# A kept block, later turns of grad_out, a fourth step of sums, bf16 spreads and earlier products in a spectral and bilinear layer's forward and backward kernel

## The chip, the core and the metric

The kernel is one program on one core of a Trainium2 chip: one launch computes the forward result and all gradients. The metric is the device time of one execution in microseconds. Three runs of the kernel before gave 1506.52, 1510.41 and 1510.88 us, so the median is 1510.41. A separate execution was profiled. Engine names below: PE is TensorE, DVE is VectorE, ACT is ScalarE, POOL is GpSimd; SP is SyncE, which issues most DMAs. Each engine runs its instructions in the order of its own queue.

## The reference, cut to what matters

```python
def _A_ref(x, w_r, w_i):                     # spectral filter
    X = jnp.fft.rfft2(x.astype(jnp.float32), axes=(-2, -1)) * (w_r + 1j * w_i)
    return jnp.fft.irfft2(X, s=(S, D), axes=(-2, -1)).astype(jnp.bfloat16)

def _B_ref(x, w_gate, w_up, w_down):         # bilinear gated unit, no nonlinearity
    g = jnp.einsum('bsd,df->bsf', x, w_gate)
    u = jnp.einsum('bsd,df->bsf', x, w_up)
    return jnp.einsum('bsf,fd->bsd', g * u, w_down)

mod = (_silu(c) @ w_mod).reshape(1, 6, 1, 576)
sa, ca, ga, sb, cb, gb = (mod[:, i] for i in range(6))
h = _layernorm(x) * (1 + ca) + sa
x = x + ga * _A_ref(h, A_w_r, A_w_i)
h = _layernorm(x) * (1 + cb) + sb
x = x + gb * _B_ref(h, B_w_gate, B_w_up, B_w_down)
```

S = 2048, D = 576, F = 4608, all tensors bf16. The outputs are x and the gradients, by `jax.vjp` with `grad_out`, of x, of the two filter weights, of the three matrices of block B, of c and of w_mod. The gradient of w_mod (`out_8`) is silu(c) times the gradient of each of the six rows of `mod`: six blocks of 576 x 576. The gradient of c is a sum of w_mod times those rows.

## The kernel before, in words

The Fourier transforms are matmuls with tables. Rows of x stand in 16 tiles of 128 (`NT`), F in 36 blocks of 128 (`NFB`), the frequencies in 19 chunks (`NCH`). The stages follow each other, each a software pipeline, whose steps are functions of a tile or chunk: `pipeline(n, [step0, step1, ...])` runs step i on tile k - i in round k.

- **Head and s1**: the six rows of `mod` are made from w_mod by matmuls (`mod_make`; `MSA`, `MCA`, `MGA`, `MSB`, `MCB`, `MGB` number them), with the gate's own column form `gbT` by the small matmuls of L487. `s1_norm`, `s1_cols` and `s1_rows` do the first layernorm and the forward transform. `grad_out` is loaded in three parts, gonA (tiles 0 to 3), gonB (4 to 7) and gonC (8 to 15), and turned on PE (L524), as fillers in this stage; L525 multiplies each turned tile by the gate into `goT`.
- **s2 and s3**: filter, inverse transform, second layernorm (`s3_norm`; L665 and what follows make `h2p`). Between their steps, and after them, run the groups of `u4_group`: for a block of F, ghhT = w_down x goT (L541 to L546), four groups of four row tiles. Groups are numbered; four make block `fb = g // 4`. ACT and DVE evacuate them from PSUM to the SBUF tile `ghh_st`, and after the fourth group POOL stores it to DRAM, `ghhT_d` (L549). The last stretch, 205 to 264.8 us, has these groups alone; at the same time SP and POOL load and transpose what the main loop needs first.
- **Main loop**, 264.8 to about 1215 us: 36 blocks. A block makes gate and up values (`gup`, L799 and L804), loads its ghhT block (`ghh`, L865, pool of two), makes the three products hhT, ggT and guT on DVE (L808 to L810), and from these the gradient of h (`u8p`, L840; its sums on DVE, L843 and L845) and of the weights (`u57p`, L737).
- **t1, t2, t3**: the backward pass through the second layernorm, the spectral block and the first layernorm. Between the steps PE gets fillers, dealt out by hand by `deal`: held matmuls of the weight gradients (`u57p`), then those of the output projection (`u3p`, L1375). `deal` also fixes the order on PE and, in t1, on ACT. `diag` (L1005) collects sums over rows in PSUM, `csA` to `csE`: diagonals are the gradients of the scale rows, an additional column that of the shift rows. `norm_back` (L964 to L974) is the layernorm's backward step; its ScalarE operation is `u` (L964).
- **Tail**: what is left of the projection, 428 matmuls in 16 tiles with `of` (L1388 to L1393) made from each, and six `section`s, one for each row of `mod`: a row's sums are spread over all partitions by fp32 matmuls with ones (`spread`, L1029), copied by ACT (`dmb`, L1048), multiplied by silu(c) on ACT (L1055) and stored to `out_8`, and multiplied by a block of w_mod on DVE (`pr7`, L1061). `late` says at which tile a section starts. `hl` and `hl2` are the projection's operands, loaded by SP; `wd` is w_down, loaded by POOL.

Orders are written out where they matter: `in_order` fixes a list of instructions, `followed(mm, act)` ties a copy to its matmul, `behind` and `queued` keep an instruction behind given ones.

Of the kernel before, what the change touches and what calls it, by code (L numbers as in the profile page):

```python
# [19 lines left out]
NT = 16  # L20
S = 2048
D = 576
# [3 lines left out]
DN = 6 * DS  # L26
# [64 lines left out]
def build(ctx, tc, A_x, A_w_r, A_w_i, B_w_gate, B_w_up, B_w_down, c_in, w_mod, grad_out,  # L91
# [42 lines left out]
    def part(ap):  # L134

        return ap.rearrange("p (m c) -> p m c", m=6)[:, :, 0:DC]

    def parts(ap):

        return ap.rearrange("p t (m c) -> p t m c", m=6)[:, :, :, 0:DC]  # L140
# [5 lines left out]
    def ones_between(ap):  # L146

        nc.gpsimd.memset(ap.rearrange("p t (m c) -> p (t m) c", c=DS)[:, :, DC:DS], 1.0)
# [109 lines left out]
    h2n = h2p[:, :, 0:D]  # L258
    gcms, gons = [], []
# [9 lines left out]
    with ExitStack() as hs:  # L269
# [97 lines left out]
        def wd_load(k):  # L367
            wdn = wdn2[:, k % 2, :, :]
            rows = B_w_down[k * FB4 * 128:(k + 1) * FB4 * 128, :].rearrange("(j f) d -> f j d", f=128)
            nc.sync.dma_start(wdn[:, :, 0:D], rows)  # L370
            nc.sync.dma_start(wdn[:, :, D:DP], rows[:, :, 512:D])
# [79 lines left out]
        hTs, zts = {}, {}  # L451
# [18 lines left out]
        def s1_cols(t):  # L470
# [6 lines left out]
            if t == 3:  # L477
# [8 lines left out]
                for m in range(5):  # L486
                    nc.tensor.matmul(ps[:, 0:1], lhsT=wms[MGB][:, m, D - 128:D], rhs=sc_bf[:, m:m + 1], start=(m == 0), stop=(m == 4))  # L487
# [32 lines left out]
        for t in range(NT):  # L520
            odd = t // 4 % 2
            pt = u4ps.tile([128, 5, 128], BF, name="u4p")
            for m in range(5):
                nc.tensor.transpose(pt[:, m, :], gon(t, m * 128 if m < 4 or not odd else D - 128, 128), ident[:])  # L524
# [4 lines left out]
        def u4_group(g, eng=None):  # L529
            fb, sb4 = g // 4, g % 4  # L530
            k, j = fb // FB4, fb % FB4
# [3 lines left out]
            if sb4 == 0:  # L535
                sts[fb] = (u4w if not u4r or fb % 4 < 2 else u4r[1]).tile([128, NT, 128], BF, name="ghh_st", bufs=2)
# [11 lines left out]
            if sb4 == 3:  # L548
                stored.append(nc.gpsimd.dma_start(ghhT_d[fb * 128:(fb + 1) * 128, :], sts[fb][:].rearrange("f t p -> f (t p)")).ins)  # L549
# [9 lines left out]
        with ExitStack() as rc:  # L559
            c2 = pool("hc2", 2, "right", stack=rc)  # L560
            hwm = pool("hwm", 2, "right", stack=rc)
# [50 lines left out]
            def s2_fill(ci):  # L612
                u4_groups(2)
                if ci == 1:
                    for j in (MGA, MSB):
                        wms[j] = mod_load(j, hwm)
                for j, c0 in ((MGA, 4), (MSB, 7), (MCB, 10)):
                    if ci == c0:
                        mod_make(j, wms[j], "a")
                if ci == 4:  # L620
                    wms[MCB] = mod_load(MCB, hwm)
# [28 lines left out]
        def s3_norm(sa):  # L650
# [13 lines left out]
            nm = hw2.tile([128, 2, D], BF, name="nm", bufs=1)  # L664
            nc.vector.tensor_tensor(out=parts(nm[:]), in0=parts(n2[:]), in1=twice(modh[MCB][:]).rearrange("p t (m c) -> p t m c", m=6), op=MUL)  # L665
# [809 lines left out]
```

## Time and profile before

| | us |
|---|---|
| median of three runs | 1510.41 |
| lowest and highest | 1506.52, 1510.88 |
| the profiled execution, its own time | 1514.57 |
| its span in the profile | 1512.8 |
| mean granted clock of TensorE | 0.994 |

The span by stage, from the busy times of each engine in windows (us):

| stage | from, to | PE | DVE | ACT | DMA share |
|---|---|---|---|---|---|
| head and s1 | 0, 64 | 56.08 | 36.74 | 41.51 | 0.90 |
| s2 | 64, 130 | 65.96 | 46.69 | 42.98 | 0.69 |
| s3 | 130, 205 | 75.00 | 51.16 | 56.74 | 1.02 |
| u4 alone | 205, 264.8 | 55.78 | 21.68 | 16.66 | 1.17 |
| end of the loop and t1 | 1215, 1320 | 100.05 | 74.55 | 52.95 | 0.85 |
| t2 | 1320, 1380 | 60.00 | 51.86 | 47.27 | 0.67 |

How to read the lines that follow in the prediction. In a timeline a line gives the start, the busy time, the engine, the line of the code, the operation with its output and inputs, the number of instructions put together, and in brackets the idle time of that engine just before, with what ended it. In the list of waits a line names who waited for whom, the total, the number of waits and the longest. In the groups a line gives total busy time and mean nanoseconds of one instruction. In windows "(x569)" is the number of instructions. A DMA line ends with the median time from its issue to the landing of the data. The DMA share of a window is the mean busy share of 16 DMA engines as counted from their packets; it can come out above 1.

### The profile page before, as it was taken

The numbers are of one execution on the slowest core, as the hardware profiler recorded it, in microseconds if no ns is written. First come the engines' busy times: TensorE is split into PE (matmuls) and PEld (weight loads), VectorE is DVE, ScalarE is ACT, GpSimd is POOL, SyncE is SP. The second block draws the span as 40 slices with busy tenths as digits, with TensorE's granted clock in tenths as the row PEclk, the third lists the DMA queues.
The fourth block names the chain that finished last, engine by engine and source line by source line (L and its number), as shares of the span: only waits on it lengthen the run. The fifth ranks groups of instructions, "written<-read, shape, count | busy, mean of one in ns | idle before, by whom it ended". The sixth has DMA issues, their size and how long they took to land.

```text
span 1512.8 us, 29102 instructions
## 1 busy us (share of the span) xinstructions
PE 1484.5 (98%) x11199; PEld 1010.2 (67%) x11199; DVE 1047.7 (69%) x2613; ACT 580.0 (38%) x1198; POOL 242.7 (16%) x376
## 2 busy tenths in 40 slices
PE   8999998999999999999999999999999999999998
PEld 6665543567667666666666676666666667788776
DVE  6476762667767666777677677677676768588884
ACT  5667752322222222222222222222222226686763
POOL 1011221102111111111111120110110113221013
PEclk9999999999999999999999999999999999999999
DMA  9868999887968769678679778689686678975687
GB/s 326 285 206 222 285 246 176 176 163 167 164 132 170 146 138 167 137 147 176 121 152 157 136 167 155 127 162 151 142 174 128 133 192 251 275 263 163 181 276 221
DMA packets 499229, 278.05 MB, mean 184 GB/s; under 512 B 423057, under 2 KB 470674, under 8 KB 498066
## 3 DMA queue, kind: packets, MB, share of 16 engines
q1 hardware_dynamic: 470690, 172.16, 55.9%
q0 software_dynamic: 28400, 104.03, 24.2%
q8 instruction: 87, 1.43, 0.4%
q14 instruction: 52, 0.43, 0.1%
HBM read 106.34 MB, written 82.21 MB: 125 GB/s over the span
## 4 chain that ended last, share of the span: by engine, by line
PE 87%; DMA 6%; DVE 3%; ACT 2%; issue 2%; SPq 0%; POOL 0%; POOLq 0%; DVEq 0%; ACTq 0%
PE u57p L737 28%; PE u8p L840 19%; PE gup L804 17%; PE u4p L546 9%; PE u3p L1375 4%; PE gup L799 3%; DMA wmj<-in_w_mod_dram 2%; DMA ghhT_d<-ghh_st 1%; PE zp L475 1%; PE yp L221 1%; DMA gonA<-in_grad_out_dram 1%; ACT w L971 1%; DVE w L966 1%; DMA n2c<-n_d 1%; PE zp L1122 1%
## 5 line engine op out<-in xcount | busy, mean ns | idle before, releaser
L845 DVE TENSOR_TENSOR acc<-acc,u8p 128x288 f32<-128x288 f32 (+1 forms) x1088 | 483.3, 453 | 276.1 <-PE u8p L840 272.3
L840 PE MATMUL u8p<-wT,ggT 128*128 128x288 bf16 x1152 | 328.0, 286 | 1.7 <-DVE acc L845 1.6
L840 PE MATMUL u8p<-wT,guT 128*128 128x288 bf16 x1152 | 327.6, 286 | 0.0
L804 PE MATMUL gup<-h2T,wgu 128*128 128x512 bf16 x1152 | 297.8, 379 | 0.0
L739 ACT CAST so<-u57p 128x288 bf16<-128x288 f32 x216 | 86.4, 400 | 530.9 <-PE u57p L737 519.1
L737 PE MATMUL u57p<-h2p,gu_sf 128*128 128x288 bf16 x1152 | 186.4, 286 | 0.0
L737 PE MATMUL u57p<-h2p,gg_sf 128*128 128x288 bf16 x1152 | 185.9, 286 | 0.0
L804 PEld LDWEIGHTS <-wgu 128*128 128x128 bf16 x1152 | 109.6, 98 | 97.9 <-issue 17.1
L840 PEld LDWEIGHTS <-ggT 128*128 128x128 bf16 x1152 | 112.6, 98 | 66.5 <-issue 14.0
L546 PE MATMUL u4p<-goT,wdT 128*128 128x512 bf16 x668 | 155.3, 383 | 0.0
L840 PEld LDWEIGHTS <-guT 128*128 128x128 bf16 x1152 | 112.7, 98 | 57.6 <-issue 2.4
L1375 PE MATMUL u3p<-wd,hl 128*128 128x288 bf16 x936 | 140.8, 287 | 2.0 <-DMA wd<-in_B_w_down_dram 2.0
L806 ACT CAST gT<-gup 128x512 bf16<-128x512 f32 x144 | 84.5, 587 | 131.6 <-PE gup L804 126.6
L737 PEld LDWEIGHTS <-hh_sf 128*128 128x128 bf16 x1152 | 112.7, 98 | 28.4
L737 PEld LDWEIGHTS <-gu_sf 128*128 128x128 bf16 x1152 | 112.5, 98 | 28.5
L737 PEld LDWEIGHTS <-gg_sf 128*128 128x128 bf16 x1152 | 112.5, 98 | 28.2
L1375 PEld LDWEIGHTS <-hl 128*128 128x128 bf16 x1152 | 107.7, 98 | 26.8 <-issue 2.1
L806 ACT CAST uT<-gup 128x512 bf16<-128x512 f32 x144 | 84.5, 587 | 77.2 <-PE gup L804 77.1
L546 PEld LDWEIGHTS <-wdT 128*128 128x128 bf16 x668 | 63.2, 99 | 73.7 <-issue 8.6
L737 PE MATMUL u57p<-gonC,hh_sf 128*128 128x288 bf16 x576 | 99.7, 286 | 0.0
L817 POOL DMA_DIRECT2D hhT_d<-hhT x36 | 33.3, 925 | 373.6 <-DVE hhT L808 350.6
L173 ACT CAST ghh_st<-u4p 128x512 bf16<-128x512 f32 x96 | 54.7, 590 | 61.4 <-PE u4p L546 42.3
(391 smaller groups left out, 1819.8 us busy)
## 6 DMA issues: line engine op xcount, KB each, us to landing
ghhT_d<-ghh_st POOLq DMA_DIRECT2D x36, 512.0 KB, 5.2
ghh<-ghhT_d POOLq DMA_DIRECT2D x36, 512.0 KB, 8.3
hhT_d<-hhT POOLq DMA_DIRECT2D x36, 512.0 KB, 6.4
hl<-hhT_d SPq DMA_DIRECT2D x28, 576.0 KB, 7.2
out_dram<-woT SPq DMA_DIRECT2D x70, 128.0 KB, 2.0
wdn<-in_B_w_down_dram SPq DMA_DIRECT2D x18, 288.0 KB, 4.4
wd<-in_B_w_down_dram POOLq DMA_DIRECT2D x36, 144.0 KB, 4.7
out_dram<-so SPq DMA_DIRECT2D x36, 144.0 KB, 2.9
```

Of the source, the lines that this page charges most:

```text
L173: nc.scalar.copy(dst, src)
L221: nc.tensor.matmul(yps[p_][:, 0:DF], lhsT=ut[:, 128 * pl:128 * pl + 128], rhs=IF[:, 3 * p_ + k, :], start=(k == 0), stop=(k == 2))
L546: nc.tensor.matmul(pt[:], lhsT=wdTs[k][:, j, m, :], rhs=goT[:, 4 * sb4:4 * sb4 + 4, m, :], start=(m == 0 and n == 5), stop=(m == n - 1))
L737: mm = nc.tensor.matmul(pw[0][:, 0:288], lhsT=sf[:, t, :], rhs=rhs_n(t, h * 288, 288), start=(t == 0), stop=(t == NT - 1))
L739: followed(mm, nc.scalar.copy(so[:, h * 288:(h + 1) * 288], pw[0][:, 0:288]))
L799: nc.tensor.matmul(pts[-1][:], lhsT=wgu[r, 8, jw * 128:(jw + 1) * 128], rhs=h2T[r, 4 * sb4:4 * sb4 + 4, 4, :], start=True, stop=False)
L804: nc.tensor.matmul(pts[k][:], lhsT=wgu[:, 4 * wi_ + m, jw * 128:(jw + 1) * 128], rhs=h2T[:, ts_, m, :], start=False, stop=(m == 3))
L806: nc.scalar.copy((gT, uT)[wi_][:, th_, :], pts[k][:])
L817: nc.gpsimd.dma_start(hhT_d[:, :, fb, :].rearrange("tp f x -> f tp x"), hhT[:].rearrange("f (tp ti) p -> f tp (ti p)", ti=2))
L840: nc.tensor.matmul(pu[:, 0:288], lhsT=l_, rhs=r_, start=(k == 0), stop=(k == len(mms) - 1))
L845: summed[t] = nc.vector.tensor_tensor(out=ghb(t)[:, hs_] if fbs[-1] == NFB - 1 else dst, in0=dst, in1=pu[:, 0:288], op=ADD).ins
L1375: mm = nc.tensor.matmul(p2[ti][:, 0:288], lhsT=hls[fb // 9][:, fb % 9, ti * 128:(ti + 1) * 128], rhs=w[:, fb - f0, h * 288:(h + 1) * 288], ...
```

## The change

Seven things are changed.

1. **Block order and a kept block.** `u4_group` takes the blocks of w_down rotated: group k of two blocks uses rows of pair (k + 1) mod 18, so that computed block fb is block fb + 2 of the main loop, the one before the last is block 1, and the last is block 0. The last stays in SBUF: it is written into the tile `ghh0`, which the main loop reads, so it is neither stored nor loaded. `ghhT` tiles of odd blocks have a pool of their own (`ghq`).
2. **Turns of grad_out behind the gate.** The first turn is ordered behind the last matmul of L487.
3. **Small storage changes.** `hwm` has one buffer and its three loads stand three chunks ahead of each use; the tile `nm` is gone, h2 is made in place; rows of n1 and n2 are 608 elements long instead of 588.
4. **t1.** ACT's order puts a step's own copies ahead of the fillers' casts, and the norm's `u` between the two; the spread of `dgb` moves here from the tail (fp32); two late transposes and a store on SP move behind later loads.
5. **t3.** The sums are a fourth step of the pipeline (`t3_sums`), `upb` has a PSUM bank to itself, and the spreads of dcb, dga and dsbr (as bf16, `ones_b`), their copies, and the products with silu(c) of four rows, on DVE instead of ACT, with their stores to `out_8`, are done here.
6. **Tail.** Only the rows dca and dsar are spread (bf16) and multiplied here; sections start one tile earlier, and three buffers hold blocks of w_mod.
7. **Sums' rows** that were held as fp32 (`dcb`, `dga`, `dca`, the shift rows) are bf16 now.

```diff
@@ u4_group
-            k, j = fb // FB4, fb % FB4
+            k, j = fb // FB4, fb % FB4 if fb < NFB - FB4 else NFB - 1 - fb
-                sts[fb] = (u4w if ...).tile([128, NT, 128], BF, name="ghh_st", bufs=2)
+                sts[fb] = ghh0 if fb == NFB - 1 else (u4w if ...).tile([128, NT, 128], BF, name="ghh_st", bufs=2)
-            if sb4 == 3:
-                stored.append(nc.gpsimd.dma_start(ghhT_d[fb * 128:(fb + 1) * 128, :], ...).ins)
+            if sb4 == 3 and fb < NFB - 1:
+                b_ = fb + 2 if fb < NFB - 2 else 1
+                stored.append(nc.gpsimd.dma_start(ghhT_d[b_ * 128:(b_ + 1) * 128, :], ...).ins)
@@ wd_load
+            p_ = (k + 1) % (NFB // FB4)
@@ main loop
-                ghh = ghp.tile([128, NT, 128], BF, name="ghh")
-                with later(1, fb):
-                    nc.gpsimd.dma_start(ghh[:]..., ghhT_d[fb * 128:(fb + 1) * 128, :])
+                ghh = ghp[fb % 2].tile([128, NT, 128], BF, name="ghh") if fb else ghh0
+                with later(1, fb) if fb else ExitStack():
+                    if fb:
+                        nc.gpsimd.dma_start(ghh[:]..., ghhT_d[fb * 128:(fb + 1) * 128, :])
@@ turns of grad_out
-                nc.tensor.transpose(pt[:, m, :], ...)
+                turn = nc.tensor.transpose(pt[:, m, :], ...)
+                if t == 0 and m == 0:
+                    in_order([gates[0], turn.ins])
@@ s3_norm
-            nc.vector.tensor_tensor(out=parts(nm[:]), in0=parts(n2[:]), in1=..., op=MUL)
+            nc.vector.tensor_tensor(out=h2..., in0=parts(n2[:]), in1=..., op=MUL)
@@ deal (t1)
-                    acts += [then_act[i_.name] for i_ in seq[last_:] if i_.name in then_act]
-                    acts += scaled["2"][k + 2:k + 3] * (at == steps and k > 0)
+                    own, fill = ([then_act[i_.name] for i_ in part_ if i_.name in then_act] for part_ in (ins, seq[last_ + len(ins):]))
+                    acts += own + scaled["2"][k + 2:k + 3] * (at == max(1, steps - 1) and k > 0) + fill
@@ spread
-        def spread(lhs, src): ...
+        def spread(d, rows=None):
+            for h in range(2):
+                k = slice(h * 288, (h + 1) * 288)
+                pp = ps_fp.tile([128, 512], FP32, name="spp", tag="fp")
+                mm = nc.tensor.matmul(pp[:, 0:288], lhsT=(ones_b if rows is None else ones_f)[:], rhs=(d if rows is None else rows)[:, k], start=True, stop=True)
+                followed(mm, nc.scalar.copy(d[:, k], pp[:, 0:288]))
+        def row_of(x, d):
+            for m in range(6):
+                ...
+                nc.vector.tensor_scalar(out=x[:, m * DC:m * DC + DC], in0=mask, scalar1=d[:, m:m + 1], scalar2=None, op0=MUL)
+        def product_rows(j, m, d):
+            ...
+            nc.vector.tensor_scalar(out=o8[r, m, :], in0=d[r, :], scalar1=sc_col[r, m:m + 1], scalar2=None, op0=MUL)
+            if m == 4:
+                nc.sync.dma_start(out_8[0:512, j * D:(j + 1) * D]..., o8[:, 0:4, :])
+                nc.sync.dma_start(out_8[512:576, j * D:(j + 1) * D], o8[64:128, 4, :])
@@ section
-            dmb = secp.tile([128, D], FP32, name="dmb", bufs=2)
-            for h in range(2):
-                nc.scalar.copy(dmb[:, h * 288:(h + 1) * 288], halves[h]())
-            wmj = secp.tile([128, 5, D], BF, name="wmj", bufs=2)
+            wmj = secp.tile([128, 5, D], BF, name="wmj", bufs=3)
-                nc.scalar.activation(out=o8[r, m, :], in_=dmb[r, :], func=ACT.Copy, scale=sc_col[r, m:m + 1])
@@ t1
+            def t1_last(t):
+                t1_rows(t)
+                if t == NT - 2:
+                    spread(dgb, dgb_l)
-            for t, k in zip((5, 6, 7, 9, 9, 11, 11, 13, 13, 15), (0, 1, 3, 4, 5, 6, 7, 8, 9, 10)):
+            for t, k in zip((5, 6, 7, 9, 9, 11, 11, 15, 15, 15), (0, 1, 3, 4, 5, 6, 7, 9, 8, 10)):
-                nc.vector.tensor_copy(dgb, dgb_l[:])
@@ t3
+        outs = [(j, m, d) for j, d in ((MGB, dgb), (MCB, dcb), (MGA, dga), (MSB, dsbr)) for m in range(5)]
-            upb = ps_fp.tile([128, 512], FP32, name="upb", tag="fp")
+            upb = ps_cs.tile([128, 512], FP32, name="upb", tag="csB")
+            if sa in (4, 7, 10, 13):
+                filter_grad(rest[sa // 3 - 1])
+            if sa == 7:
+                row_of(dsbr, dsb)
+            if sa in (2, 6, 10):
+                spread((dcb, dga, dsbr)[sa // 4])
+            for _ in range({0: 3, 1: 2}.get(sa % 4, 0)):
+                if outs:
+                    product_rows(*outs.pop(0))
+        def t3_sums(sa):
+            if sa == 0:
+                add_zero(csD, csE)
+            diag(csD, csE, 0, ghr3[:, sa % 3, :], n1cs[sa % 5][:], DS, DC + 1, sa == NT - 1)
-        pipeline(NT, [t3_rows, t3_cols, t3_norm], 3)
+        pipeline(NT, [t3_rows, t3_cols, t3_norm, t3_sums], 3)
@@ tail
-        late = {8: (MSB, of_sums(dsb)), 9: (MCB, of_rows(dcb)), 10: (MGA, of_rows(dga)), 11: (MGB, of_rows(dgb)), 12: (MSA, of_sums(dsa)), 13: (MCA, of_rows(dca))}
+        late = {9: [(MCB, dcb)], 10: [(MSB, dsbr), (MGA, dga)], 11: [(MGB, dgb), (MSA, dsar)], 12: [(MCA, dca)]}
+                    if t in (8, 9):
+                        j, d = ((MCA, dca), (MSA, dsar))[t - 8]
+                        with behind([mm.ins, ld3["last"]]):
+                            spread(d)
+                            for m in range(5):
+                                product_rows(j, m, d)
```

More of the change, by code (lines that the diff above doesn't have):

```diff
@@ L258, in build @@
     h2n = h2p[:, :, 0:D]
+    ghpcm = tc.tile_pool(name="ghp", bufs=1, reuse_waits="tile")
+    ghp = [ghpcm.__enter__()]
+    ghh0 = ghp[0].tile([128, NT, 128], BF, name="ghh")
     gcms, gons = [], []
@@ L486, in s1_cols @@
                 for m in range(5):
[L487 removed]
+                    mm = nc.tensor.matmul(ps[:, 0:1], lhsT=wms[MGB][:, m, D - 128:D], rhs=sc_bf[:, m:m + 1], start=(m == 0), stop=(m == 4))
+                gates.append(mm.ins)
                 nc.vector.tensor_copy(gbT[64:128, 1, 4:5], ps[64:128, 0:1])
@@ L1147, in build @@
             dsb = diag_sums(tl, csA, csB, 0, "dsb")
-            with behind([i_ for i_ in nc.cur_bb.bb.instructions[-40:] if i_.engine == mybir.EngineType.DVE][-1:]):
-                nc.vector.tensor_copy(dgb, dgb_l[:])
         c1acm.__exit__(None, None, None)
```

87 lines of the change are left out of this document (35 added, 52 removed).

## The prediction

> **What bounds the kernel now.** I read the page first, then the waits of TensorE, then windows by stage, and only then the timelines of the stages that the change touches.
>
> ```profile
> span 1512.8 us, 29102 instructions
> PE 1484.5 (98%) x11199; PEld 1010.2 (67%) x11199; DVE 1047.7 (69%) x2613; ACT 580.0 (38%) x1198; POOL 242.7 (16%) x376
> ```
>
> TensorE is busy for 1484.5 of 1512.8 us, so everything that is not matmul work is worth 28.3 us at most.  A change can win only by closing some of those 28 us, by taking PE work out, or by lifting the clock. The waits of PE say where the gaps are (columns: total, times, longest):
>
> ```profile
> PE u4p L541 <- ACT ghh_st L173: 4.0, 1, 4.0
> PE u4p L524 <- DMA gonA<-in_grad_out_dram: 2.4, 1, 2.4
> PE u3p L1375 <- DMA wd<-in_B_w_down_dram: 2.0, 1, 2.0
> ...
> PE zp L1122 <- ACT b_Vp L1131: 1.3, 7, 0.2
> ...
> PE spp L1029 <- ACT dmb L1048: 1.3, 2, 0.8
> ```
>
> By stage (PE, PEld, DVE, ACT, POOL busy, granted clock, DMA share, GB/s):
>
> ```profile
> 264.80:1215.00 950.20, 950.20 (x6811) 641.06 (x6812) 669.16 (x1577) 244.96 (x482) 133.14 (x171) 1.00 0.78 152
> ...
> 1446.00:1512.80 66.80, 57.89 (x438) 44.09 (x435) 43.03 (x121) 31.47 (x55) 18.55 (x30) 0.97 0.84 259
> ```
>
> The main loop has no gap at all, and the change leaves its PE work alone. So the result is decided in the other 560 us, stage by stage. Nearly every span term below counts one to one on the end, because PE sets it.
>
> **1. Turns of grad_out behind the gate.** The 16 turns (L524) are fillers in the head. The first one waits for gonA:
>
> ```profile
> 16.36 1.42 PE L475 MATMUL zp<-RDs,hT 128*128 128x292 bf16 x10 [0.32 <-ACT hT L173]
> ...
> 20.57 0.23 PE L524 MATMUL u4p<-ident,gonA 128*128 128x128 bf16 x1 [2.40 <-DMA gonA<-in_grad_out_dram]
> ...
> 21.01 1.57 PE L524 MATMUL u4p<-ident,gonA 128*128 128x128 bf16 x14
> 22.38 2.48 PE L475 MATMUL zp<-RDs,hT 128*128 128x292 bf16 x10
> ...
> 29.27 0.28 PE L487 MATMUL modc<-sc_bf,wm 128*128 128x1 bf16 x5
> ```
>
> The wait is 2.40, and the ten matmuls after it take 2.48 instead of 1.42, so the event costs 3.5. The changed order puts the gate's matmul of L487 (at 29.27) ahead of the first turn, when the load has landed. But the turns are not removed. About twenty of them, at 0.11 each (1.57 for 14), slide out of the head into the start of the second stage, where PE has matmuls of its own all the time: +2.2. And the head also hangs on the norm's chain (0.32 for ACT's hT in the first row), so part of the 2.4 may come back as that wait. Bounds -3.5 and +2.2; I take -1.5, nearer to the gain because the wait itself surely goes.
>
> The Trainium skill, page "TensorE: Matmul & The Clock Gate", section "Why this matters for your kernels", says that idle gaps of more than about 3 us lose the clock. The rows above show a slow clock after a gap of 2.40. By that rule the event would cost 2.4 alone, and the sum would end about 1 us higher; the row decides.
>
> **2. Block order and the kept block.** ghhT is made in 36 blocks, each stored by POOL and reloaded by the main loop. Towards the end the DMA engines are full:
>
> ```profile
> 214.10 22.50 DMA ghhT_d<-ghh_st
> ...
> 229.69 3.63 PE L546 MATMUL u4p<-goT,wdT 128*128 128x512 bf16 x16
> 237.33 1.31 PE L541 MATMUL u4p<-goT,wdT 64*128 64x512 bf16 x4 [4.02 <-ACT ghh_st L173]
> 238.57 5.80 PE L546 MATMUL u4p<-goT,wdT 128*128 128x512 bf16 x16
> ```
>
> One store took 22.5 us to land, its buffer stayed taken, ACT could not evacuate, and PE stood for 4.02. Then sixteen matmuls took 5.80 instead of 3.63, 2.2 more, and in that ratio the four before them 0.5 more: 6.7 in all. The change drops one store and one 512 KB load (the one below), and moves the next load behind the last store:
>
> ```profile
> 220.01 0.57 POOL L865 DMA_DIRECT2D ghh<-ghhT_d  x1
> ```
>
> It ran beside the late store, so taking it away helps. But the store was issued at 214.10, and the transposes that fill the queues stay. Bounds 0 and -6.7; I take -3, near the middle, since neither end has a row of its own.
>
> Against that stands block 1. It is now computed second to last, so its store (262.02 in this trace) must land before its load is issued, and VectorE needs it at 278.85 in block 1 of the main loop:
>
> ```profile
> ghhT_d<-ghh_st POOLq DMA_DIRECT2D x36, 512.0 KB, 5.2
> ghh<-ghhT_d POOLq DMA_DIRECT2D x36, 512.0 KB, 8.3
> ...
> 262.02 0.53 POOL L549 DMA_DIRECT2D ghhT_d<-ghh_st  x1 [3.53 <-DMA wT<-in_B_w_gate_dram]
> ...
> 278.85 0.42 DVE L809 TENSOR_TENSOR ggT<-ghh,uT 128x512 bf16<-128x512 bf16 x1
> ```
>
> By the medians it lands at 262.0 + 5.2 + 8.3 = 275.5, 3.3 early. With the store of 22.5 above it would be at 292.8, 14 late. Behind the waiting ggT on VectorE stand the copies of u8p, and PE needs their buffers. Bounds 0 and +14; I take +1.
>
> **3. Smaller moves that cost nothing here.** One buffer less for w_mod blocks with later loads and makes, h2 without its own nm tile (the same three VectorE operations), and rows of 608 instead of 588 all lie under u4 matmuls that keep PE full; if that cover goes they cost well under 1 us.
>
> **4. t1.** In the steps whose fillers carry ScalarE casts, `so` stands in front of the norm's u and b_Vp, and PE's zp waits. Starts of zp with and without those casts:
>
> ```profile
> 1278.14 0.54 PE L1122 MATMUL zp<-T_RF,gyT 128*128 128x292 bf16 x3
> 1282.49 0.54 PE L1122 MATMUL zp<-T_RF,gyT 128*128 128x292 bf16 x3
> ...
> 1291.25 0.91 PE L1122 MATMUL zp<-T_RF,gyT 128*128 128x292 bf16 x6
> 1295.26 0.91 PE L1122 MATMUL zp<-T_RF,gyT 128*128 128x292 bf16 x6
> ```
>
> 4.35 against 4.01 a step. The change queues a step's own copies first and the fillers' casts last, so seven steps (the seven waits of zp above) win 0.34 each: -2.4. What may be late next is the so cast, whose PSUM buffer the fillers want, and the wd wait of 2.0, which follows loads paced by the step. Bounds 0 and -4.4 (the wd wait gone too). The spread of dgb is added, two fp32 halves; one such spread is 1.13 in the tail (row in part 6): +1.1. It replaces a copy on VectorE, and dgb's five products then take that copy's place behind t1:
>
> ```profile
> 1322.93 1.85 DVE L1149 COPY dgb<-dgb_l 128x576 f32<-128x576 f32 x1
> ```
>
> At 0.37 a product (part 5) they take 1.9, as long as the copy: 0. Net -1.3.
>
> **5. t3.** The sums become a fourth step, upb gets its own bank, six bf16 half-spreads, their copies and 15 products join. Now VectorE, not PE, paces this stage:
>
> ```profile
> 1387.13 0.92 PE L221 MATMUL yp<-T_IF,ut 128*128 128x289 bf16 x6
> 1390.66 0.92 PE L221 MATMUL yp<-T_IF,ut 128*128 128x289 bf16 x6
> ...
> 1400.02 0.46 DVE L974 TENSOR_TENSOR ob<-u,w 128x576 bf16<-128x576 bf16 x1 [0.58 <-ACT w L971]
> 1400.39 0.46 DVE L224 TENSOR_TENSOR ghr<-yp,ye 128x289 bf16<-128x289 f32 x1
> ...
> 1403.77 0.46 DVE L974 TENSOR_TENSOR ob<-u,w 128x576 bf16<-128x576 bf16 x1 [0.58 <-ACT w L971]
> ...
> L973 DVE TENSOR_SCALAR w<-n2c,ab 128x576 bf16<-128x576 bf16 x16 | 6.8, 426 | 0.0
> ```
>
> The first tiles go at 3.53, PE's own pace, the later ones at 3.75, with one VectorE wait of 0.58 a tile for ScalarE's w. A product is the operation of L973, 0.43 long; operations that follow each other on VectorE start 0.37 apart (1400.02 to 1400.39), so 15 x 0.37 = 5.6. dsb's six pieces of 96 columns cost at most 0.37 each, 2.2, and I take half: 6.7 on the engine that paces. The products fall on six tiles, and each tile hides 0.58 of them: -3.5. That leaves +3.2; PE no longer stands behind gh's sums, which become a step of their own, so I take +3. Bounds 0 (all in gaps; six copies of 0.4 on ScalarE lie in its own waits) and +7.8 (none).
>
> The Trainium skill, page "VectorE: DVE Perf Modes", section "The TRN2 errata — SBUF-src ops pay a fixed extra latency per instruction", gives 58 cycles and a quarter cycle an element at 0.96 GHz, which is 0.21 for 576. The row of L973 has 0.43, twice that. By the page the 15 products would take 3.2 and the sum would be 2.4 lower.
>
> **6. Tail.** Six sections each spread a row by fp32 matmuls (L1029), wait, and copy; after that the sections' products:
>
> ```profile
> 1452.97 1.13 PE L1029 MATMUL spp<-dcb,ones_f 128*128 128x288 f32 x4
> ...
> 1500.71 4.57 PE L1375 MATMUL u3q<-wd,hl 128*128 128x288 bf16 x36
> ...
> 1496.01 0.76 DVE L1061 SCALAR_TENSOR_TENSOR pr<-wmj,dmb 128x576 bf16<-128x576 bf16 x1 [13.94 <-DMA wmj<-in_w_mod_dram]
> ...
> 1507.16 0.45 DVE L1392 TENSOR_TENSOR of<-u3q,gb_h 128x288 bf16<-128x288 f32 x1
> ```
>
> Six spreads x 1.13 = 6.8 leave PE, with the 1.3 of waits on spp listed above; four bf16 halves at 4.57 / 36 = 0.13 come: -7.6. PE's other work there is unchanged. PE's last projection ends at 1505.28, but VectorE reads it only at 1507.16, since ten pr products had waited 13.94 for a late w_mod block. The sections start one tile earlier with a third buffer, and four of six blocks' out_8 stores have left the stage, so those products end before PE does: -1.5 of the 1.9. Against it: SyncE's queue is in order, and hl loads now stand behind out_8's store of MCA, which waits for VectorE's products.
>
> ```profile
> 1476.12 2.61 SPq L1168 DMA_DIRECT2D hl<-hhT_d  x2
> ...
> hl<-hhT_d SPq DMA_DIRECT2D x8, 576.0 KB, 8.5
> ```
>
> A tile of hl takes 8.5 to land; if its issue slips by that much PE stands for up to 8.5. Bounds 0 and +8.5; I take +1.5, near 0, since the list of waits has none for hl now. Net -7.6.
>
> **The sum.** -1.5 - 3 + 1 - 1.3 + 3 - 7.6 = -9.4 on the profiled execution of 1514.57 (span 1512.8 and 1.8 around it): 1505.2. That execution is 4.2 above the median of the runs, 1510.41 (1506.52 to 1510.88), so I forecast 1501.0 for the median, -0.6%.
>
> **Rivals.**
> - *Everything closes.* The late store's stall goes whole (-6.7), the head wins 3.5, t3 hides the products (0), t1 -1.3, the tail -9.1, no late loads: -20.6, 1489.8. For it: all these waits are single events with one cause each. Against: the transposes that made the store late stay.
> - *Given back.* The store's stall stays (0), the head gives nothing (0), t3 pays 6.7, block 1 costs 1, t1 wins 1.3 and the tail's hl loads take back 4 of 9.1, so 5.1: +1.3, 1511.7. For it: VectorE already paces t3, and the DMA share of the tail is 0.84. Against: it needs four terms to miss on the same side.
> - *Slower: block 1's round trip.* Store and load in the saturated stretch stop VectorE in the second block of the main loop, and PE with it. With 14 late and 2.7 of slow clock (what the stall at 237.33 cost beyond its 4.02) it is +16.7 in place of +1: -9.4 + 15.7 = +6.3, 1516.7. It decides from 12.2 late: with the 2.7 that is 14.9, the 10.4 that the rest of the sum gains and the 4.5 that a measurement can tell. For it: a store of 22.5 in this very stretch. Against: the median is 5.2, and the queues empty when the main loop starts.
> - *The change doesn't do what it says*: the turns could stay where they are, or all 36 stores still be issued. The changed code orders the first turn behind the gate and issues 35 stores, so it has no share of its own.
>
> **Chances.** Forecast 0.52 (its own range 1494 to 1505), everything closes 0.12, given back 0.19, slower 0.17. About 0.3% (4.5 us) is what a measurement can tell from no change. The first two are faster, 0.64; given back is within, 0.19; the last slower, 0.17. The 8-in-10 range takes in the first rival's time and most of given back: 1489 to 1515.
>
> **What would show it.** PE's wait on gonA and the one on ghh_st gone, with zp at 1.42 throughout; no wait of VectorE for ghh in block 1; zp in t1 at 4.01 in all steps; yp in t3 up to 4.5 apart on product tiles; no f32 spp in the tail, and the last of at PE's end. It is wrong if a new PE wait over 3 us appears for hl, wd or ghh, or if t3 grows by more than 7.8.

## The result, and the profile after

| | before | changed |
|---|---|---|
| median (us) | 1510.24 of 20 runs | 1498.18 of 20 runs |
| lowest and highest | 1503.41, 1531.64 | 1494.53, 1508.15 |
| ratio changed to before, 95% interval | | 0.9913 (0.9887 to 0.9938) |
| profiled execution, its time | 1514.57 | 1508.15 |

The change saves 12.1 us, 0.9%; the forecast for the median was 1501.0. The profiled execution is the slowest of the changed kernel's 20, 10 us above their median. So its trace probably holds a loss that a median run does not have. The page of the changed kernel begins:

```profile
span 1506.3 us, 29074 instructions
...
PE 1473.0 (98%) x11189; PEld 1004.3 (67%) x11189; DVE 1054.0 (70%) x2642; ACT 557.2 (37%) x1168; POOL 243.0 (16%) x381
```

PE has 11.5 us less work than before (1484.5), but the span is only 6.5 shorter: 5.0 of new idle time stand against it. The list of PE's waits of the changed kernel names it (total, times, longest):

```profile
PE u4p L549 <- DMA wdT<-wdn: 9.7, 1, 9.7
PE u3p L1394 <- DMA wd<-in_B_w_down_dram: 2.8, 1, 2.8
...
PE yp L222 <- ACT dsbr L1039: 1.7, 1, 1.7
...
PE csD L1012 <- DVE ghr L225: 1.3, 1, 1.3
...
PE yp L222 <- ACT dga L1039: 0.8, 1, 0.8
```

The waits for gonA, for `ghh_st`, for `b_Vp` and for `dmb` are gone, as the prediction wanted. One of 9.7 for a transposed block of w_down is new, and of t3's three waits in this list (`yp` twice, `csD` once) two are for copies of the added spreads.

The next table cuts the span at the same PE instructions in each kernel: the start of the last row of inverse-transform matmuls (`yp`) of s3, the first `gup`, the last `csB` of t1, the first `yp` of t3, the end of its last `csE`, the end of the last `u3q`, and the last `of`. The column e1 is the same changed kernel, profiled again in a later experiment.

| stretch (us) | before | changed | e1 |
|---|---|---|---|
| head to s3 | 201.56 | 200.09 | 200.18 |
| u4 alone | 63.23 | 68.54 | 56.26 |
| main loop and t1 | 1056.60 | 1053.51 | 1051.47 |
| t2 | 61.17 | 62.17 | 62.16 |
| t3 | 61.41 | 62.34 | 62.35 |
| tail, to the end of PE's projection | 61.31 | 53.26 | 53.25 |
| the last `of` behind it | 1.88 | 0.04 | 0.04 |
| rest | 5.64 | 6.35 | 5.59 |
| span | 1512.8 | 1506.3 | 1491.3 |

**Where it was lost: u4 alone.** PE's timeline of the changed kernel:

```profile
228.22 3.63 PE L554 MATMUL u4p<-goT,wdT 128*128 128x512 bf16 x16
...
241.52 1.04 PE L549 MATMUL u4p<-goT,wdT 64*128 64x512 bf16 x4 [9.67 <-DMA wdT<-wdn]
242.49 5.72 PE L554 MATMUL u4p<-goT,wdT 128*128 128x512 bf16 x16
```

A stall of the same form as before the change, with another transfer at its head: a gap of 9.67, then four matmuls in 1.04 and sixteen in 5.72 instead of 3.63. The stretch is 12.3 longer than e1's 56.26.

**Head, t1 and t3.** PE's timeline of the changed kernel, further on:

```profile
22.50 1.42 PE L480 MATMUL zp<-RDs,hT 128*128 128x292 bf16 x10
...
25.80 0.28 PE L492 MATMUL modc<-sc_bf,wm 128*128 128x1 bf16 x5
...
26.72 0.39 PE L530 MATMUL u4p<-ident,gonA 128*128 128x128 bf16 x4
...
1276.59 0.92 PE L1127 MATMUL zp<-T_RF,gyT 128*128 128x292 bf16 x6
...
1280.60 0.92 PE L1127 MATMUL zp<-T_RF,gyT 128*128 128x292 bf16 x6
...
1323.42 1.16 PE L1038 MATMUL spp<-dgb_l,ones_f 128*128 128x288 f32 x4
...
1429.03 0.54 PE L222 MATMUL yp<-T_IF,ut 128*128 128x289 bf16 x3 [1.67 <-ACT dsbr L1039]
```

The gate's matmuls (25.80) stand ahead of the first turns (26.72), with no wait, and ten zp keep 1.42. In t1 these two steps start 4.01 apart. The spread of dgb has moved here at 1.16. In t3, PE waits 1.67 for a PSUM bank that a spread's copy on ACT still holds.

DVE's timeline of the changed kernel has three rows for t3 and the end:

```profile
1402.02 0.46 DVE L981 TENSOR_TENSOR ob<-u,w 128x576 bf16<-128x576 bf16 x1 [0.31 <-ACT w L978]
...
1412.98 1.21 DVE L1054 TENSOR_SCALAR o<-dga,sc_col 128x576 bf16<-128x576 bf16 x4
...
1499.95 0.46 DVE L1411 TENSOR_TENSOR of<-u3q,gb_h 128x288 bf16<-128x288 f32 x1 [3.33 <-PE u3q L1394]
```

Four products in a row take 1.21; each is 0.37 long, so they start 0.28 apart. DVE's wait ahead of `ob` is 0.31 on this tile where it was 0.58. The last `of` starts 0.04 after PE's last matmul ends, instead of 1.88.

**Tail.** The window of the tail and the DMA groups of 1440 to 1500 us (median time to landing last) of the changed kernel show less traffic:

```profile
1446.65:1499.91 53.26, 53.22 (x434) 42.07 (x432) 44.58 (x128) 7.51 (x18) 18.98 (x29) 1.00 0.85 260
```

```profile
hl<-hhT_d SPq DMA_DIRECT2D x9, 576.0 KB, 7.5
...
wmj<-in_w_mod_dram SPq DMA_DIRECT2D x6, 576.0 KB, 6.2
...
out_dram<-o SPq DMA_DIRECT2D x2, 576.0 KB, 4.6
```

PE is busy for 53.22 of 53.26, with no fp32 spread in it. Two stores of `o` (these are `out_8`) are in this time; the same view of the kernel before has six, with 9.2 to landing for `wmj`:

```profile
wmj<-in_w_mod_dram SPq DMA_DIRECT2D x6, 576.0 KB, 9.2
...
out_dram<-o SPq DMA_DIRECT2D x6, 576.0 KB, 8.4
```

### The profile page after: what moved, and what is told of

It reads as the page before. It is cut to its first block, busy times and chain, and to the rows that moved or that the text cites. A ratio compares the mean times of both kernels' runs of the same rounds, so it can differ in the third digit from the quotient of the medians.

```text
span 1506.3 us, 29074 instructions
## 1 busy us (share of the span) xinstructions
PE 1473.0 (98%) x11189; PEld 1004.3 (67%) x11189; DVE 1054.0 (70%) x2642; ACT 557.2 (37%) x1168; POOL 243.0 (16%) x381
## 4 chain that ended last, share of the span: by engine, by line
PE 87%; DMA 5%; DVE 4%; issue 2%; ACT 1%; POOL 1%; SPq 0%; POOLq 0%; DVEq 0%
PE u57p L743 28%; PE u8p L846 19%; PE gup L810 17%; PE u4p L554 10%; PE u3p L1394 4%; PE gup L805 3%; PE yp L222 1%; DMA wdT<-wdn 1%; DMA h2p<-in_A_x_dram 1%; DMA gonA<-in_grad_out_dram 1%; PE zp L480 1%; DMA out_dram<-woT 1%; PE upa L215 1%; DVE pr L1066 1%; DMA woT<-so 1%
```

## The experiments

The theory: the tail makes most of the gain, t1's order the next part, and the u4 stretch is settled by how transfers happen to land in each execution. The rivals: the kept block makes the gain; bf16 alone makes the tail's; the stall at `wdT` belongs to the change's own order of loads. Each kernel is the changed one with one edit, except e9, which is the kernel before with one edit. The medians of the kernel before next to them were 1507.6 (e1 to e4), 1509.22 (e5 to e8), 1509.74 (e9 to e11) and one run of 1502.55 (e12).

### e1: the changed kernel again

> The changed kernel itself, a second profile of it. Theory: the 9.7 us wait of PE for the transposed w_down is a chance of that one execution (the DMA engines are full from 205 to 265 us, and which transfer is late changes from run to run), so it is gone or of another size here, while the stages outside of 205 to 268 us repeat within 0.3 us. Rival: it is built into the changed order of the queues; then it comes back at 9 to 10 us in the same place. Time: about 0.991 of the kernel before.

Measured: 1493.86 (1492.95 to 1498.29, 6 runs), ratio 0.9899 (0.9859 to 0.9939). One of PE's waits in its profile:

```profile
PE u3p L1394 <- DMA wd<-in_B_w_down_dram: 0.9, 1, 0.9
```

No wait for `wdT`, and u4 alone takes 56.26. The same instructions lost 12.3 in one execution and nothing in another. The wait for `wd` in t1 varies as well, 0.9 against 2.8. t2, t3 and the tail agree to 0.01 in these two, so of the late stages only they can be read from a single profile.

### e2 and e5: all 36 blocks stored and loaded

```diff
-            p_ = (k + 1) % (NFB // FB4)
+            p_ = k
-            k, j = fb // FB4, fb % FB4 if fb < NFB - FB4 else NFB - 1 - fb
+            k, j = fb // FB4, fb % FB4
-                sts[fb] = ghh0 if fb == NFB - 1 else (u4w if ...).tile(...)
+                sts[fb] = (u4w if ...).tile(...)
-            if sb4 == 3 and fb < NFB - 1:
+            if sb4 == 3:
...
```

The rest of the two edits, left out here, loads block 0 like the others. Both have the old block order. e2 also takes back the pool of two for `ghh` in the main loop; e5 keeps the two pools and their places in SBUF.

> The changed kernel with the old block order: all 36 blocks stored and loaded, no tile kept. Theory of the prediction: keeping one block takes 3 us of stall away, so this is about 3 us slower than the changed kernel, 0.993 of the kernel before, with a stall of ghh_st of some 4 to 7 us. Rival: one store and one load of 40 transfers in a saturated stretch change nothing on average; then it is 0.991 like the changed kernel, and the stall before the main loop is between 0 and 12 us by chance in both.

> The changed kernel with all 36 blocks computed in order, stored and loaded, but with the changed kernel's places in SBUF (the tile of block 0 is loaded instead of kept). The second run had another layout, and its 9.9 us wait for wd in t1 may belong to that. Theory (the kept block relieves the queues before the main loop): the stretch from the end of s3 to the first gup grows from 56.3 to 60 to 69 in most executions, t1 stays at the changed kernel's 1051.5 to 1053.5, and the ratio to before is 0.994 to 0.997. Rival (the layout, not the block, cost the second run its time): the stretch is 56.3 again and the ratio 0.990.

Measured: e2 1513.55 (1504.3 to 1520.81, 12 runs), ratio 1.0017 (0.9988 to 1.0047). e5 1497.09 (1493.98 to 1508.74, 12 runs), ratio 0.9921 (0.9887 to 0.9956). e2 alone would say that the kept block makes the whole gain; e5, with the same stores, has all of the gain within what its runs can tell. PE's waits and POOL's timeline of e2:

```profile
PE u4p L546 <- DMA wdT<-wdn: 10.9, 1, 10.9
PE u3p L1389 <- DMA wd<-in_B_w_down_dram: 9.9, 1, 9.9
```

```profile
1290.92 0.55 POOL L1098 DMA_DIRECT2D gx_d<-gxr  x1 [1.32 <-DVE gxr L976]
1305.64 0.55 POOL L1098 DMA_DIRECT2D gx_d<-gxr  x1 [14.18 <-DVE gxr L976]
1309.20 0.54 POOL L1098 DMA_DIRECT2D gx_d<-gxr  x1 [3.02 <-DVE gxr L976]
1310.09 0.90 POOL L1171 DMA_DIRECT2D wd<-in_B_w_down_dram  x1 [0.35 <-issue]
```

and POOL's timeline of the changed kernel at the same place:

```profile
1291.95 0.55 POOL L1103 DMA_DIRECT2D gx_d<-gxr  x1 [2.96 <-DVE gxr L981]
1298.16 0.90 POOL L1176 DMA_DIRECT2D wd<-in_B_w_down_dram  x1 [5.66 <-DMA n2c<-n_d]
```

In e2 the load of `wd` stands behind two more stores of `gx_d` on POOL's queue, each of which waits for a tile of t1; PE then waits 9.9 for it. In e5, which stores all blocks too but keeps the pools, the load is issued ahead of them again, at 1290.00, and the wait is 2.8. So most of e2's loss in main loop and t1 (1065.50) comes from a queue that its pools moved, not from the block.

e5's u4 stretch had no stall (56.27), e2's had one of 10.9, so storing all blocks does not bring the stall each time. Yet it fills the DMA queues. The DMA groups of this stretch, before (205 to 264 us), in e1 and in e5 (205 to 256), one fence for each:

```profile
ghhT_d<-ghh_st POOLq DMA_DIRECT2D x13, 512.0 KB, 11.7
ghh<-ghhT_d POOLq DMA_DIRECT2D x2, 512.0 KB, 17.1
```

```profile
ghhT_d<-ghh_st POOLq DMA_DIRECT2D x13, 512.0 KB, 5.1
```

```profile
ghhT_d<-ghh_st POOLq DMA_DIRECT2D x13, 512.0 KB, 11.1
```

and ACT's timeline of e5 at the start of the main loop:

```profile
261.51 0.58 ACT L811 CAST gT<-gup 128x512 bf16<-128x512 f32 x1 [5.51 <-DMA ghhT_d<-ghh_st]
```

With all blocks stored, and the loads of blocks 0 and 1 in this stretch, a store takes 11 us or more to land, in e1 5. In e5 ScalarE's first cast of the main loop waits 5.51 for one of these stores; PE then waits 1.38 for that cast, its granted clock is 0.50 from 263.6 to 266.8, and the loop takes 3.6 longer to reach t1 than in e1. All four profiles with 36 stores (before, e2, e5, e9) have medians of 11 to 15 us to landing in this stretch, and in all four PE waits in the stretch or right behind it (4.0, 10.9, 1.4 and 3.1); of the ten with the kept block (medians of 4 to 9) it does in two, the changed kernel's first profile (9.7) and e11 (3.9). So the rearranged blocks do ease this stretch. Which part of it does so (the store less, or the two loads that moved out) no run separates, and the times cannot show the size: e5 against the changed kernel is 0.9921 against 0.9913, with overlapping intervals.

e5's main loop and t1 take 1059.51, where 1051.5 to 1053.5 had been expected: 3.6 of that at the loop's start, the rest in t1, with waits of 2.8 for `wd` and 0.9 for `yc` and a lower clock behind them.

### e3: the late transpose issued earlier

```diff
+        in_order([turns[15], h2Ts[2]])
```

SP issues the transpose of w_down's pair 15 ahead of the third transpose of h2 (`turns`, `h2Ts`: their DMA instructions).

> The changed kernel with one order more on SyncE: the transposed load of the w_down pair that PE waited 9.7 us for goes ahead of the third transpose of h2. Theory (the queue's order makes that pair late): the wait is gone, 9.7 + 2.6 us at most against the profiled execution and some 2 to 4 us on the median, 0.988 to 0.990 of before. Rival (saturation): some other wait of 4 to 10 us appears between 205 and 268 us, and the median stays at 0.991.

Measured: 1496.2 (1493.11 to 1515.53, 12 runs), ratio 0.9923 (0.9892 to 0.9954); u4 alone 56.26, as in e1. The queue order makes no difference that shows: eight of the ten profiles with the kept block, e1's without this order among them, have no stall there. One of its runs still took 1512.74; where it lost time was not profiled. What decides between 56 and 69 us from one execution of the same program to the next is left as chance landings on full queues; that is argued, and no run names an order that prevents it.

### e7: the turns of grad_out without their order

```diff
-                if t == 0 and m == 0:
-                    in_order([gates[0], turn.ins])
```

> The changed kernel without the order of the turns behind the gate. Theory: the end of s3 (last yp before the u4 stretch, 200.1 in the changed kernel, 201.6 before) comes 1.5 later, with a wait for gonA of about 2.4 in the head. Rival: the other changes of the first stages (buffers, h2 in place) made those 1.5, and the end of s3 stays at 200.1 to 200.4 although the wait for gonA is back.

Measured: 1496.38, one run. PE's timeline:

```profile
17.48 2.43 PE L480 MATMUL zp<-RDs,hT 128*128 128x292 bf16 x10 [0.32 <-ACT hT L174]
...
20.65 0.29 PE L530 MATMUL u4p<-ident,gonA 128*128 128x128 bf16 x1
...
27.90 0.28 PE L492 MATMUL modc<-sc_bf,wm 128*128 128x1 bf16 x5
```

The turn is back ahead of the gate, but its load was nearly in time, and the last row of s3 starts at 200.18, as in e1. In e9, with the old order and a wait of 2.1 for gonA, it starts at 199.73. What e9 lacks is the slow clock: its ten zp behind the turns take 1.40 and its granted clock is 1.00 over 15 to 40 us, where before the change they took 2.48 at 0.50 (21.2 to 24.5). The order removes the wait and does not move the end of s3.

### e6: t1's old order on ScalarE

```diff
-                    own, fill = ...
-                    acts += own + scaled["2"][k + 2:k + 3] * (at == max(1, steps - 1) and k > 0) + fill
+                    acts += [then_act[i_.name] for i_ in seq[last_:] if i_.name in then_act]
+                    acts += scaled["2"][k + 2:k + 3] * (at == steps and k > 0)
```

> The changed kernel with ScalarE's old order in t1 (fillers' casts ahead of the norm's u). Theory of the prediction: seven steps at 4.35 instead of 4.01 come back, so the stretch from the first gup to the last sum of t1 grows by 2.4, from 1051.5 (with a wd wait of 0.9) to 1053.9, less what the wd wait gives back. Rival (the wait for wd swallows it): it stays at 1051.5 plus 0 to 0.9, since wd's load is late by its own clock.

Measured: 1500.58, one run. PE's timeline and, in the next fence, its waits:

```profile
1270.00 0.54 PE L1127 MATMUL zp<-T_RF,gyT 128*128 128x292 bf16 x3
...
1274.35 0.54 PE L1127 MATMUL zp<-T_RF,gyT 128*128 128x292 bf16 x3
```

```profile
PE zp L1127 <- ACT b_Vp L1136: 1.2, 7, 0.2
```

The steps of 4.35 and the seven waits are back. Main loop and t1 take 1058.71 against 1053.51 in the changed profile, where `wd` was late by the same 2.8: 5.2, of which 7 x 0.34 = 2.4 are the steps and 1.2 a wait for `yc`. The rest lies in matmuls that ran at a lower clock after the wait for `wd` (granted 0.50 over 1298.8 to 1302.0), and that is not the order's: e5 has the new order, the same wait of 2.8, one of 0.9 for `yc` and the slow clock too. From the first `zp` of t1 to its last `csB`, e5 takes 64.5 and e6 67.3, 2.8 more: the 2.4 of the steps, and the rest the longer wait for `yc`.

### e4, e8, e10 and e11: what t3 pays

e4 orders each spread's last copy on ACT ahead of the tile's `u`; e8 takes the sums back into the norm's step (the removed `t3_sums` is not shown); e10 does fifteen products (MCB, MGA, MSB) twice; e11 is e4 with those products on GpSimd.

```diff
+                in_order([spread((dcb, dga, dsbr)[sa // 4]), scaled["1"][-1]])          # e4, and spread returns its last copy
-        pipeline(NT, [t3_rows, t3_cols, t3_norm, t3_sums], 3)                          # e8
+        pipeline(NT, [t3_rows, t3_cols, t3_norm], 3)
+            for _ in range(2 if d is not dgb and j in (MCB, MGA, MSB) else 1):          # e10
+            eng = nc.gpsimd if j in (MCB, MGA, MSB) else nc.vector                      # e11
```

> The changed kernel with ScalarE's copies of the spread rows in t3 put ahead of the norm's u instead of behind it. Theory: PE's two waits in t3 for a PSUM bank of these spreads (0.8 for dga, 1.7 for dsbr) come from the copies standing behind u, ob and w on ScalarE; they are gone, and t3 from its first to its last yp shrinks by about 2 us, 58.7 to 56.7. Rival: VectorE paces t3 as the prediction had it, so the waits only move to VectorE's results and t3 keeps its 58.7 within 0.5.

> The changed kernel with t3's sums inside the norm's step again, all products and spreads staying. Theory (a step of their own lets PE run at 3.53 a tile while VectorE is a tile behind): t3 grows from 62.3 by 2 to 4 us, near the +3 that the prediction took. Rival (VectorE paces t3 with or without that step): 62.3 within 0.5.

> The changed kernel with the 15 products of t3 (rows of MCB, MGA, MSB with silu(c)) each written twice. Theory after the eighth run (the products lie in VectorE's waits for ScalarE's w, 0.58 a tile, and beside PE's own pace): 15 more of 0.28 to 0.37, 4.2 to 5.6, find part of those waits already taken, and t3 grows from 62.35 by 2 to 4. Rival (VectorE has room for all of them): t3 stays within 0.5.

> The fourth run's kernel (copies ahead of u) with the 15 products of t3 on GpSimd, which is busy for 4 of 66 us there, instead of VectorE. Theory (the fourth run lost at the end of t3, where PE waited 2.1 for VectorE's ghr, and a slow clock after it): with the products off VectorE that wait falls below 1, and t3 and tail together go from 115.7 to 113 to 114. Rival (GpSimd and VectorE hold each other up, or ScalarE paces): 115.7 or more.

Measured, beside e1 (one run each; times 1494.56, 1494.21, 1495.22 and 1507.03):

| stretch (us) | e1 | e4 | e8 | e10 | e11 |
|---|---|---|---|---|---|
| first to last `yp` of t3 | 58.70 | 56.63 | 59.97 | 59.56 | 65.54 |
| t3 | 62.35 | 61.16 | 63.01 | 63.40 | 70.23 |
| tail, PE | 53.25 | 54.58 | 53.16 | 53.37 | 53.25 |

*e10*: fifteen more products cost 1.05, or 0.07 each; the rest goes into DVE's waits. *e8*: the fourth step of sums is worth 0.66, not the 2 to 4 of its theory. *e4*: the waits for `dsbr` and `dga` go and the `yp` come 2.07 sooner. But PE's timeline of e4 shows where that goes:

```profile
1431.85 0.26 PE L1012 MATMUL csD<-n1c,ghr 128*128 128x97 bf16 x2 [2.11 <-DVE ghr L225]
1432.42 2.37 PE L1396 MATMUL u3p<-wd,hl 128*128 128x288 bf16 x9
```

and PE's timeline of e1 has at that place:

```profile
1432.26 1.26 PE L1394 MATMUL u3p<-wd,hl 128*128 128x288 bf16 x9
```

PE comes earlier to sums that are no earlier, waits 2.11 for `ghr` instead of 1.3, and the nine matmuls behind it take 2.37 instead of 1.26. With the tail's 1.33 more nothing is left. *e11*: the groups of its profile give GpSimd 1.84 to 2.05 a product, where DVE had one every 0.28; the group of dcb:

```profile
L1057 POOL TENSOR_SCALAR o<-dcb,sc_col 128x576 bf16<-128x576 bf16 (+1 forms) x5 | 9.6, 1931 | 1.8 <-ACT dcb L1039 1.7
```

DVE's own operations became longer beside them: its timeline of e11 has this one, which takes 0.17 on the tiles without products:

```profile
1392.57 0.52 DVE L975 TENSOR_SCALAR ab<-s 128x2 f32<-128x2 f32 x1
```

t3 takes 7.9 more than in e1; how much of it these longer operations make, and how much the wait for the products, is not worked out. The rest of e11's longer time is a stall in u4 alone (61.91).

### e9: the kernel before with bf16 spreads alone

```diff
-            d = pool.tile([128, D], FP32, name=name)
+            d = pool.tile([128, 2 * D], BF, name=name)[:, 0:D]
...
-            spread(ones_f[:], ...)
+            spread(ones_b[:], ...)
```

`dgb` and `dx` likewise; the tiles keep their bytes, so that nothing else moves in SBUF.

> The kernel before with one part of the change alone: the six spreads of the tail in bf16 instead of fp32, nothing moved. Theory: the fp32 passes are most of the tail's gain, so TensorE's time from the last sum to the last u3q falls from 61.3 by 6.8 - 12 x 0.13 = 5.2 to 56.1; the waits for ScalarE's copies and the late end on VectorE (1.9) stay, so the whole is about 0.9965 of before. Rival (the place counts, not the precision): the halves stay behind ScalarE's copies and VectorE's products, the waits grow by what the matmuls lose, and the tail stays above 59.

Measured: 1511.53 (1507.41 to 1521.31, 10 runs), ratio 1.0023 (0.9988 to 1.0058): no gain. Its tail takes 67.49 on PE, 6.2 more than before. PE's waits and timeline of e9:

```profile
PE u3p L1375 <- DMA hl<-hhT_d: 5.5, 2, 4.8
...
PE spp L1029 <- ACT dmb L1048: 2.4, 1, 2.4
...
PE spp L1029 <- DVE dx L1040: 1.8, 2, 1.4
```

```profile
1486.14 2.32 PE L1375 MATMUL u3p<-wd,hl 128*128 128x288 bf16 x9 [4.76 <-DMA hl<-hhT_d]
```

PE has less to do and now waits, 9.7 in all, for the copies between spreads and for `hl`, and the nine matmuls behind the longest wait take 2.32.

### e12: fp32 rows in the changed tail

```diff
-                            spread(d)
+                            spread(d, dca_l if j == MCA else dsa_l)     # both fp32, in tiles of their own
```

> The changed kernel with the two spreads that are left in its tail (dca, dsar) in fp32 instead of bf16; places, products and the three spreads of t3 stay. Theory (a spread costs its passes on TensorE wherever nothing waits for it): the tail grows from 53.25 by 2 x (1.13 - 0.25) = 1.8 to 55.0. Rival (after the ninth run: what matters in the tail is what stands between the projection's operands and their loads): a longer chain in front of out_8's store of MCA delays the loads of hl behind it, and the tail grows by 3 or more with a wait of PE for hl.

Measured: 1511.21, one run. The tail takes 62.29, 9.0 more. PE's timeline:

```profile
1448.16 1.24 PE L1038 MATMUL spp<-dca_l,ones_f 128*128 128x288 f32 x4 [0.54 <-DVE dca_l L1023]
...
1487.97 2.34 PE L1396 MATMUL u3p<-wd,hl 128*128 128x288 bf16 x9 [5.22 <-DMA hl<-hhT_d]
```

The fp32 passes themselves are 2 x (1.24 - 2 x 0.13) = 2.0, with the prediction's 0.13 for a bf16 half; the wait for `hl` and the slow matmuls behind it are 5.22 + 1.1. The other 9 us by which this profile is longer than e1's lie in the head (2.0) and in main loop and t1 (7.1, with a wait of 3.3 for `yc`), which the edit does not aim at, so the 1511.21 is not the price of the fp32 rows. Its rows lie elsewhere in SBUF, and SP's order of the `hl` loads differs too, so precision and queue are not apart here. Whether the tail without waits, as the change's, needs the bf16 rows or the order of the loads is not shown.

## Why the prediction was right, and where its steps were off

The direction was right and the median came 2.8 below the forecast, within the range. The terms, step by step:

1. **Head, -1.5.** The pair of profiles gives -1.47. The wait on gonA went and zp kept 1.42. But e7 without the order and e9 with the old one end s3 no later than the changed kernel, so the order shows no gain of its own: the pair differs by the slow clock behind the wait, which before's profile had and e9's, with nearly the same wait, did not. "The wait itself surely goes" was true, and nothing hung on it.
2. **u4 alone, -3.** +5.3 in the profiled execution, -7.0 in e1. The weak step is the size: the term treats the late store as one event that is softened, and one profile of before cannot give that, since gaps of 0 to 10.9 come with and without the kept block, at whichever transfer is late. The direction, "taking it away helps", is borne out by the landings (5.1 in e1, 11 and more wherever all blocks are stored) and by the count of profiles that lose time there. What it is worth on average is open. The one new wait over 3 us, for `wdT`, is not among those that the prediction named as signs. **Block 1's round trip, +1**, cost nothing: neither VectorE nor PE waits for `ghh` at the start of the main loop, and the load lands 3.5 us after its issue. The rival on the slower side, which hung on it, fell.
3. **Storage changes, 0.** As forecast in the changed kernel. e2 shows what the step overlooked: other pools can also move loads on POOL's queue, and there it cost 9.9.
4. **t1, -1.3.** The steps that waited are at 4.01 now, and e6 brings 4.35 back, 2.8 more than e5 in t1 with 0.3 of it for `yc`: -2.4 is confirmed. The stretch came out -3.1 and -5.1 in the two profiles, since `wd` waited 2.8 and 0.9 and the matmuls after the first did not slow down this time. The spread of dgb made t2 1.0 longer, against +1.1.
5. **t3, +3.** +0.93. That DVE takes the products into its waits and the rest shows was right, but the term was mis-sized: products start 0.28 apart, not 0.37, and fifteen more of them cost 1.05 (e10), where the prediction let 3.2 show. The copies on ScalarE, which it put at nothing, do cost: PE waits 1.7 and 0.8 for them, and with these gone in e4 the `yp` come 2.07 sooner, though the end does not. The Trainium skill, page "VectorE: DVE Perf Modes", in the section that the prediction names, gives about 0.21 by its formula, which the section itself calls too low for a single operation; 0.28 lies between that and the row of 0.43.
6. **Tail, -7.6.** -8.05 on PE and -1.84 for the late `of`: -9.9. PE's busy time in the tail fell from 59.49 to 53.22, by 6.3, which is the sum's 6.8 less 0.5; its idle time fell by 1.8, the 1.3 listed and 0.5 for `dx`. The +1.5 for `hl` was not called: it lands in 7.5 and PE never waits for it. But that less work on PE is by itself time fell in e9: there the fp32 passes go, and the tail grows by waits. In the changed kernel the tail is free of waits; that the moved products, stores and copies make it so, and not the third buffer or the earlier sections, is argued and not tried alone.

"Given back" fell as well: t3 paid 0.9 of its 6.7, and `hl` took back nothing. That the sum came so near is in part luck. The tail and t1 gave more than forecast, t3 took less, and the execution from which the terms were read had losses that another one did not: e9, the same kernel up to the tail, has neither the slow clock in the head nor the one behind `wd`. From that profile to e1's the stages add up to -21.5, close to the first rival's -20.6. The medians differ by 12.1. The 9.4 between them are the two executions' own distance from their medians: the profiled execution of before stands 4.3 above its median, and e1's (1493.09) 5.1 below that of the changed kernel. So a single pair of profiles can be off by most of such a change. No experiment beat the changed kernel; e4 and e8 are equal to it within what one run can tell.

What stays open: what the kept block is worth in time (under what 12 and 20 runs can tell), what sets off the stall in u4 alone, how the median's 12.1 divides among the stages, and in the tail how much is precision and how much the queue.

## What to carry to other kernels

Before a wait at a full DMA queue is booked as a saving, take a second profile of the same kernel: here one stretch of unchanged instructions took 56.3 or 68.5 us. Two profiles do not settle it either: that the kept block eases the stretch showed only in the landings, over fourteen profiles. Work taken off the bounding engine is time only if what it then waits for is early too: e9 made PE's six spreads bf16 and gained nothing; the changed kernel, from whose tail four sections' copies, products and stores have gone as well, gained 8 us there. And an experiment that undoes one part must keep the pools as they are, or it measures a moved load, as e2 did.

## What the runs showed of the hardware

The clock after a gap goes by more than the gap's length. Nine matmuls took 2.37 instead of 1.26 after a wait of 2.11 in e4, and e9's took 2.32 after 4.76. But the changed kernel's wait of 2.84 for `wd` left the clock alone, where 2.0 before the change did not, and in e6 a wait of the same 2.84 for the same load did not either. The windows of before, of the changed kernel and of e6, one fence for each (granted clock third from the end):

```profile
1305.00:1310.00 5.00, 5.00 (x41) 3.59 (x39) 4.16 (x12) 3.19 (x8) 0.00 (x0) 0.70 0.43 138
```

```profile
1305.00:1310.00 5.00, 4.10 (x44) 3.42 (x44) 4.63 (x15) 2.22 (x7) 0.54 (x1) 1.00 0.91 162
```

```profile
1297.00:1302.00 5.00, 4.54 (x24) 3.04 (x24) 4.63 (x15) 1.42 (x4) 0.54 (x1) 0.67 0.59 159
```

Narrower windows show what the means hide: the clock is at 0.50 from 1304.6 to 1308.0 before the change, and in e6 from 1298.8 to 1302.0.

The Trainium skill, page "TensorE: Matmul & The Clock Gate", section "Why this matters for your kernels", puts the loss at idle gaps of more than about 3 us. These runs show it after shorter gaps, the shortest 1.38 (e5, 0.50 from 263.6 to 266.8 us), and not each time. So the 2.11 of e4 cost at least 2.11 + 1.11 = 3.2, the 2.84 of the changed kernel cost 2.84, and the price of such a wait cannot be told from its length alone.
